# A gated linear attention with a maxout feed-forward on one Trainium2 core: the hand-planned order is planned anew, with the transfers' shared semaphores in the planner and other constants

## The chip, the core and the metric

The kernel runs on one core of one Trainium2 chip. The metric is device time in microseconds (us) of one execution, as the median of the runs shown. Beside it stands the profile of one execution: its span, and what each engine did in it. TensorE is PE (its weight loads are PEld), VectorE is DVE, ScalarE is ACT, GpSimd is POOL, SyncE is SP. SP and ACT are also the two queues that issue transfers.

## The reference

Inputs are `q`, `k`, `v`, `alpha` (batch 4, 8 heads, 768 positions, head dimension 48, float32) and four weight matrices. What is computed:

```python
for t in range(768):                       # per batch and head, state is 48 x 48
    state = alpha[t][:, None] * state + outer(k[t], v[t])
    y[t] = q[t] @ state
x = y as 3072 tokens x 384
h = maximum(maximum(x @ w1, x @ w2), x @ w3)     # 384 -> 768
out = h @ w_out                                  # 768 -> 384
```

## The kernel before, in words

**Units.** The recurrence is done in blocks of 128 positions. A unit u is one block of one batch with all 8 heads; there are 24, block by block, so units 0 to 3 are the first block of the four batches. Inputs are loaded by pairs of units: pair n holds units 2n and 2n+1. For the first four pairs each of a, q, k, v (a is alpha) comes in two half loads of 192 KB, one for each unit of the pair; later pairs come in full loads of 384 KB. In memory the 48 numbers of one position and head are one run of 192 bytes, so these loads consist of small packets.

**A unit's steps.** ACT takes the logarithm of alpha (`la`, L498). PE sums it along the block (L551, one matmul) and ACT makes the two exponentials `ep` and `en` from it (L554, L556). POOL, or DVE where the table `EARLY` says so, forms `qk` = q times ep and k times en (L563); POOL or ACT scales v (L575, L570). PE turns q and k (L533, 8 transposes), DVE copies them out (`qkT`, L537). PE forms the scores (L597, 8 matmuls) and DVE masks them (`LA`, L602). PE forms the outputs from `LA` and v (L643), and, from the second block on, from the carried state `Z` (L640). ACT copies them to `xb` (L651), PE turns them (L665, 3 transposes) and DVE copies them to `xT` (L669). For the last units the two turnings are done by transfers instead: units from `CROSS_IN` on for q and k (L582), from `CROSS_OUT` on for the outputs (L657). The state is carried on by L695 on PE and L701 and L708 on DVE and POOL.

**The feed-forward.** max(x w1, x w2, x w3) is x w1 + max(0, x (w2-w1), x (w3-w1)). So the weights are prepared once: ACT casts w1 and w_out to half precision (L436), POOL or DVE forms the differences `wd` (`subs`, L445; the table `SUBS` says which engine), PE and ACT turn w1 (L463, L469) and PE folds w1 w_out (`folded`, L480, 18 matmuls), which ACT copies (L487). Each matrix comes in two pieces, `WCUTS`: part 0 is 256 columns (384 KB), part 1 is 512 columns (768 KB). For a group of one or two units PE multiplies `xT` by the two differences (L736), ACT takes the positive part (L747), DVE the maximum (L752), and PE multiplies back (L769, 9 matmuls a unit: 3 with the folded matrix, 6 with w_out). ACT copies the result and issues the store (L780, L781). `SINGLE` and `LAST` say how many units at the start and at the end form groups of their own; the others go two by two. One unit alone takes 36 matmuls of 128 columns in L736, two together 36 of 256 columns.

**What sets the order.** Nothing is scheduled by the compiler: every step is entered into `Plan` with an engine, a cost and a rank, and `Plan.order` plays them through (each engine takes the ready step with the earliest start, then the lowest rank), with a small account of transfers (`Transfers`) and of the TensorE clock (`Clock`). The order it finds is emitted as it stands; each engine then runs its own list strictly in order. `FIRST` is the order in which the first loads (`load`, on SP, L406) and the weight pieces (`wload`, on ACT, L427) are asked for. A weight piece is held back in the plan until the load `BACK` + 1 places before it in `FIRST` has landed. `LEAD` holds the ranks of the first feed-forward groups (unit number plus lead).

**The shared semaphores.** The transfers of both queues take eight semaphores in turn, in the order in which they are emitted; call the transfers #0, #1, #2 and so on. Transfer #n waits, on the queue that issues it, until #(n-8) has landed, unless that queue has waited for this already. In the built program before, w3's first piece is #28 on ACT and waits for #20, the k of unit 3. The plan before does not know of this.

Of the kernel before, what the change touches and what calls it, by code (L numbers as in the profile page):

```python
# [25 lines left out]
QUEUES = ("SP", "ACT")  # L26
DMA_IN = {"SP": 0.9, "ACT": 0.9}
DMA_OUT = {"SP": 0.9, "ACT": 0.9}
DMA_BOTH = {"SP": 0.2, "ACT": 0.8}
SPARE = 1.5  # L30
LEAD = (2.5, 8.0, 6.5, 8.0)
EARLY = {0: ("POOL", "POOL", "POOL"), 2: ("POOL", "DVE", "POOL"), 3: ("POOL", "POOL", "POOL"),
         4: ("POOL", "POOL", "POOL"), 5: ("POOL", "POOL", "ACT"), 6: ("POOL", "POOL", "POOL"),
         7: ("POOL", "DVE", "POOL"), 9: ("DVE", "POOL", "POOL"), 10: ("POOL", "POOL", "POOL")}
WCUTS = (0, 256, 768)
SUBS = {(1, 0): "DVE", (1, 1): "POOL", (2, 0): "DVE", (2, 1): "DVE"}
FIRST = (("w", 0, 0), ("a", 0, 1, 2), ("k", 0, 1, 2), ("k", 1, 0, 1), ("q", 0, 0, 1),
         ("q", 0, 1, 2), ("a", 0, 0, 1), ("k", 0, 0, 1), ("a", 1, 0, 1), ("q", 1, 0, 1),
         ("v", 1, 0, 1), ("w", 0, 1), ("w", 1, 1), ("w", 3, 0), ("v", 0, 0, 1), ("w", 1, 0),
         ("w", 3, 1), ("v", 0, 1, 2), ("qav", 1, 1, 2), ("w", 2, 0), ("k", 1, 1, 2),  # L40
         ("w", 2, 1), ("a", 2, 0, 1), ("vk", 2, 0, 1), ("q", 2, 0, 1), ("a", 2, 1, 2),
         ("a", 3, 1, 2), ("vq", 2, 1, 2), ("k", 2, 1, 2), ("a", 3, 0, 1), ("q", 3, 0, 1),
         ("k", 3, 0, 1), ("k", 3, 1, 2), ("q", 3, 1, 2), ("v", 3, 1, 2), ("v", 3, 0, 1))
WARM = (-1, 0, 0)
BACK = 3
SINGLE, LAST = 4, 2
PAIRS, WIDE = 10, 99
CROSS_IN, CROSS_OUT = 22, 18
FETCH, FETCHES, STORE = 1.0, (25.0, 10.2), 0.3
CLOCK_WINDOW, CLOCK_PHASE, CLOCK_WAKE, CLOCK_KEEP = 3.413, 0.0, 0.75, 0.37  # L50

# [70 lines left out]
class Plan:  # L122
# [55 lines left out]
    def order(self):  # L178
# [19 lines left out]
                pending[self.steps[i][0]].add(i)  # L198
        free = dict(dict.fromkeys(HOP, 0.0), SP=SP_FIRST)
        held = {"DVE": 0.0, "POOL": 0.0}  # L200
        bank_free = {b: 0.0 for b in range(NBANKS)}
        place, seq, clock = {}, [], Clock()
        dma, mode, fetch = Transfers(), 0, FETCHES[0]

        def finish(i, done):
            for k in owner.get(i, ()):
                left[k] -= 1
                last[k] = max(last[k], done)
                if not left[k]:
                    for j in range(self.width.get(k, 1)):  # L210
                        bank_free[place[k] + j] = last[k]
            for j in after[i]:
                arrive(j, done)
# [7 lines left out]
        while len(seq) < n:  # L221
            best = None
            for e, cand in pending.items():
                pick = None
                for i in cand:
                    at = self.homes(bank_free, self.steps[i][5])
                    if at is None:
                        continue
                    t = max(ready[i], free[e], at[0])
                    if e == "POOL" or e == "DVE" and self.steps[i][7]:  # L230
                        t = max(t, held["DVE" if e == "POOL" else "POOL"])
                    turn = TURN_RANK if e == "PE" and self.steps[i][7] != mode else 0.0
                    key = (t, self.steps[i][2] + turn, i)
                    if pick is None or key < pick:
                        pick = key
                if pick is not None and (best is None or pick < best[0]):
                    best = (pick, e)
            if best is not None and best[0][0] > fetch:
                dma.store(FETCH)
                fetch += FETCHES[1]  # L240
            landing = dma.next()
            if landing and (best is None or landing[0] <= best[0][0]):
                end, i = dma.next(commit=True)
                self.landed[i] = end
                finish(i, end)
                continue
            (t, _, i), e = best
            _, cost, _, _, _, banks, load, m, late = self.steps[i]
            pending[e].discard(i)
            for k, b in self.homes(bank_free, banks)[1].items():  # L250
                place[k] = b
                for j in range(self.width.get(k, 1)):
                    del bank_free[b + j]
            if e == "PE":
                if m != mode:
                    mode = m
                    cost += TURN_COST
                cost = clock.run(t, cost)
            free[e] = t + cost
            if e == "POOL" or e == "DVE" and m:  # L260
                held[e] = t + cost
            seq.append((t, i))
            if load > 0 and e in QUEUES:
                dma.add(e, t + cost + DMA_IN[e], load, i, late)
            else:
                if load < 0:
                    dma.store(-load)
                finish(i, t + cost + HOP[e])
            if i in follows:
                arrive(follows[i], t)  # L270
# [5 lines left out]
def kernel(  # L276
# [12 lines left out]
    nc = tc.nc  # L289
# [3 lines left out]
    DF = moe_w_out.shape[0]  # L293
# [80 lines left out]
    plan = Plan({x: range(NBANKS) for x in ("Lp", "hp", "tp", "A", "yp", "xp", "pp", "gp", "op", "wt", "wp", "wm")})  # L374
# [23 lines left out]
    asked = []  # L398
# [19 lines left out]
    casting = {g: tuple(x[2] for x in FIRST if x[:2] == ("w", g)) for g in (0, 3)}  # L418
# [3 lines left out]
        return t[:, lo // P:hi // P, :] if g == 3 else t[:, :, lo:hi]  # L422

    def wload(g, part):
        gate = [asked[-1 - BACK]] if len(asked) > BACK else []
        plan.step("ACT", 0.8, -1.0,
                  lambda: nc.scalar.dma_start(  # L427
                      piece(wst[g], g, part),
                      piece(matrices[g].rearrange("(t p) f -> p t f", p=P), g, part)),
                  reads=gate + ([("ws room", p) for p in casting[0]] if g == 3 else []),  # L430
                  writes=[("ws", g, part)], line="weights",
                  load=3.25 * (WCUTS[part + 1] - WCUTS[part]) / DF)
        if g in (0, 3):
            n = NFT * (WCUTS[part + 1] - WCUTS[part])
            plan.step("ACT", 0.2 + 0.00083 * n, -0.5,
                      lambda: nc.scalar.copy(out=piece((w1h, 0, 0, wo16)[g], g, part),  # L436
                                             in_=piece(wst[g], g, part)),
                      reads=[("ws", g, part)],
                      writes=[("w", g, part)] + [("ws room", part)] * (g == 0))
# [277 lines left out]
    def ffn(f, units):  # L717
        k = len(units)
# [6 lines left out]
        for q in range(NJ // span):  # L725
            js = range(q * span, (q + 1) * span)
            parts = sorted({p for j in js for p in parts_of(j // 2)})
            for g in range(2):
                r = rank[2 * q + g]
# [25 lines left out]
        for i in range(k):  # L755
            m = units[i]
# [32 lines left out]
            def leave_left(m=m, ok=ok, rows=rows):  # L789
                nc.scalar.copy(out=obs[m % 4][:, left], in_=live[ok][:, left])  # L790
                nc.scalar.dma_start(rows[:, left], obs[m % 4][:, left])

            plan.step("ACT", 0.7, r, leave_left, reads=[ok], writes=[("ob room", m % 4)])
            plan.step("DVE", 0.3, r,
                      lambda m=m, ok=ok: nc.vector.tensor_copy(out=obs[m % 4][:, right],
                                                               in_=live[ok][:, right]),
# [1 line left out]
            plan.step("SP", 0.4, r,  # L798
                      lambda m=m, rows=rows: nc.sync.dma_start(rows[:, right],
                                                               obs[m % 4][:, right]),  # L800
                      reads=["right"], writes=["done"])


    for what, n, lo, *hi in FIRST:
# [74 lines left out]
```

## Time and profile before

| | |
|---|---|
| time, median of 3 runs | 160.46 us (160.32 to 161.14) |
| time of the profiled execution | 159.96 us |
| its span | 158.2 us |
| busy: PE, DVE, ACT, POOL | 133.3, 94.4, 85.1, 76.4 us |
| loads of q, k, v, alpha | 20.09 MB on SP's queue (with the little that else goes there), 104080 packets |
| weights and stores | 9.44 MB on ACT's queue, 6944 packets |

The span is what the profile shows between the first and the last instruction; 1.8 us of the profiled execution's time lie outside of it. In the rows of the profile, a line such as L736 is a line of the kernel before; "busy, mean ns of one" and the idle time in front of an instruction are given with what ended it. The chain of waits is followed back from the last instruction; its pieces add up to the span.

### The profile page before, as it was taken

The numbers are of one execution on the slowest core, as the hardware profiler recorded it, in microseconds if no ns is written. First come the engines' busy times: TensorE is split into PE (matmuls) and PEld (weight loads), VectorE is DVE, ScalarE is ACT, GpSimd is POOL, SyncE is SP. The second block draws the span as 40 slices with busy tenths as digits, with TensorE's granted clock in tenths as the row PEclk, the third lists the DMA queues.
The fourth block names the chain that finished last, engine by engine and source line by source line (L and its number), as shares of the span: only waits on it lengthen the run. The fifth ranks groups of instructions, "written<-read, shape, count | busy, mean of one in ns | idle before, by whom it ended". The sixth has DMA issues, their size and how long they took to land.

```text
span 158.2 us, 4216 instructions
## 1 busy us (share of the span) xinstructions
PE 133.3 (84%) x1686; PEld 105.8 (67%) x1686; DVE 94.4 (60%) x162; ACT 85.1 (54%) x175; POOL 76.4 (48%) x105
## 2 busy tenths in 40 slices
PE   0217270599999999999999999999999999999991
PEld 0105160596877777869778878869788796979680
DVE  7004640334669898988769957969678750923130
ACT  3355300789378628655865936856748455343330
POOL 0044490100653642969596949699985940000000
PEclk9999999999999999999999999999999999999999
DMA  6999999898999998999989999999521691122121
GB/s 125 255 215 358 227 303 279 205 323 164 199 237 263 205 237 185 234 227 242 230 173 289 181 257 268 176 247 227 110 102 32 59 245 47 57 50 99 54 99 50
DMA packets 111043, 29.80 MB, mean 188 GB/s; under 512 B 104624, under 2 KB 109872, under 8 KB 111024
## 3 DMA queue, kind: packets, MB, share of 16 engines
q1 hardware_dynamic: 104080, 20.09, 66.0%
q10 hardware_dynamic: 6944, 9.44, 18.3%
q8 instruction: 13, 0.21, 0.6%
q14 instruction: 6, 0.05, 0.1%
HBM read 23.69 MB, written 4.72 MB: 180 GB/s over the span
## 4 chain that ended last, share of the span: by engine, by line
PE 71%; SPq 11%; DVE 7%; DMA 6%; issue 2%; ACT 1%; ACTq 0%; DVEq 0%
PE psum L736 29%; PE psum L769 20%; SPq L406 11%; DMA kn<-in_k_dram 6%; PE psum L533 5%; PE psum L597 3%; PE psum L643 3%; DVE LA L602 2%; PE psum L551 2%; PE psum L640 2%; PE psum L480 2%; PE psum L665 2%; PE psum L695 2%; DVE Z L708 2%; DVE qkT L537 1%
## 5 line engine op out<-in xcount | busy, mean ns | idle before, releaser
L736 PE MATMUL psum<-xT,wd 128*128 128x256 f16 (+1 forms) x540 | 55.3, 255 | 0.1
L736 PEld LDWEIGHTS <-wd 128*128 128x128 f16 x540 | 43.9, 100 | 5.1 <-issue 0.5
L563 POOL TENSOR_TENSOR qk<-qn,ep 128x384 f16<-128x384 f32 x23 | 23.0, 1000 | 32.2 <-ACT ep L554 30.3
L602 DVE TENSOR_TENSOR LA<-psum,c 128x1024 f16<-128x1024 f32 x24 | 28.5, 1220 | 12.2 <-PE psum L597 12.2
L752 DVE TENSOR_TENSOR hT<-psum,hT 128x512 f16<-128x512 f32 (+1 forms) x39 | 24.4, 645 | 15.0 <-PE psum L736 9.0
L747 ACT ACTIVATE hT<-psum 128x512 f16<-128x512 f32 (+1 forms) x39 | 21.6, 570 | 18.2 <-PE psum L736 17.7
L769 PE MATMUL psum<-wo,hT 128*128 128x384 f16 x144 | 27.5, 326 | 0.0
L563 POOL TENSOR_TENSOR qk<-kn,en 128x384 f16<-128x384 f32 x22 | 22.4, 1021 | 9.3 <-ACT en L556 9.1
L537 DVE COPY qkT<-psum 128x1024 f16<-128x1024 f16 x22 | 15.1, 688 | 13.4 <-PE psum L533 11.7
L651 ACT ACTIVATE xb<-psum,c 128x384 f16<-128x384 f32 x24 | 13.8, 582 | 16.8 <-DMA kn<-in_k_dram 11.6
L780 ACT COPY ob<-psum 128x384 f32<-128x384 f32 x23 | 11.0, 478 | 20.7 <-PE psum L769 20.7
L769 PEld LDWEIGHTS <-hT 128*128 128x128 f16 x144 | 14.0, 98 | 9.2
L533 PE MATMUL psum<-c,qk 128*128 128x128 f16 x176 | 15.1, 231 | 5.9 <-POOL qk L563 5.9
L708 POOL TENSOR_TENSOR Z<-U,G 48x192 f16<-48x192 f32 x32 | 15.6, 504 | 3.4 <-DVE U L701 2.5
L575 POOL TENSOR_SCALAR v<-vn,c 128x384 f16<-128x384 f32 x23 | 13.8, 603 | 7.0 <-DMA vn<-in_v_dram 6.7
L533 PEld LDWEIGHTS <-qk 128*128 128x128 f16 x176 | 11.5, 103 | 8.3 <-POOL qk L563 7.7
L769 PE MATMUL psum<-w1o,xT 128*128 128x384 f16 x72 | 15.6, 326 | 0.0
L554 ACT ACTIVATE ep<-psum 128x384 f32<-128x384 f32 x24 | 11.9, 494 | 6.2 <-PE psum L551 5.1
L669 DVE COPY xT<-psum 128x384 f16<-128x384 f16 x18 | 6.3, 353 | 10.1 <-PE psum L665 9.9
L556 ACT ACTIVATE en<-psum 128x384 f32<-128x384 f32 x24 | 11.9, 496 | 0.0
L665 PE MATMUL psum<-c,xb 128*128 128x128 f16 x54 | 6.3, 234 | 6.6 <-ACT xb L651 6.6
L643 PE MATMUL psum<-v,LA 128*128 128x48 f16 x192 | 11.6, 188 | 0.1
(41 smaller groups left out, 143.7 us busy)
## 6 DMA issues: line engine op xcount, KB each, us to landing
out_dram<-ob ACTq DMA_DIRECT2D x23, 192.0 KB, 3.1
an<-in_alpha_dram SPq DMA_DIRECT2D x8, 384.0 KB, 5.9
qn<-in_q_dram SPq DMA_DIRECT2D x8, 384.0 KB, 5.7
kn<-in_k_dram SPq DMA_DIRECT2D x8, 384.0 KB, 6.3
vn<-in_v_dram SPq DMA_DIRECT2D x8, 384.0 KB, 6.1
ws<-in_moe_w_dram ACTq DMA_DIRECT2D x3, 768.0 KB, 7.5
an<-in_alpha_dram SPq DMA_DIRECT2D x8, 192.0 KB, 4.9
kn<-in_k_dram SPq DMA_DIRECT2D x8, 192.0 KB, 4.2
```

The costliest lines, as they stand in the source:

```text
L406: nc.sync.dma_start(t[:, lo:hi], views[x][cb * P:(cb + 1) * P, g * HG + lo:g * HG + hi])
L533: nc.tensor.transpose(live[tk][:, w, j, :], qk[:, w, 2 * j:2 * j + 2, :], ident)
L537: plan.step("DVE", 0.69, u, lambda: nc.vector.tensor_copy(out=qkT, in_=live[tk]), reads=[tk], writes=[("qkT", u % 3)])
L563: nc.gpsimd if eng == "POOL" else nc.vector).tensor_mul(
L575: lambda: nc.gpsimd.tensor_scalar(out=v16, in0=ld["v"][n % 5][:, hs], scalar1=vsc, scalar2=1.0, op0=AOP.mult, op1=AOP.mult),
L602: lambda: nc.vector.tensor_mul(LA.rearrange("p a b t -> p (a b) t"), live[Ak].rearrange("p a (b t) -> p (a b) t", t=P), maskA.unsqueeze(1) ...
L643: nc.tensor.matmul(yp[:, 2 * j + p, :], LA[:, p, j, :], v16[:, 2 * j + p, :], start=(cb == 0), stop=True, skip_group_check=True)
L708: eng.tensor_mul(Zn[rows, :, cols], U[rows, :, cols], G[rows, i * NP:(i + 1) * NP].unsqueeze(2).broadcast_to([D, NP, D]))
L736: nc.tensor.matmul(live[gk][:, jj, :], wd[:, kt, g, j * P:(j + 1) * P], xT[:, kt, :], start=(kt == 0), stop=(kt == NFT - 1))
L747: lambda h=h, gk=gk: nc.scalar.activation(out=h, in_=live[gk], func=AFT.Relu),
L752: lambda h=h, gk=gk: nc.vector.tensor_max(h, live[gk], h),
L769: nc.tensor.matmul(live[ok], a[:, i * P:(i + 1) * P], w, start=(kt == 0), stop=(kt == nk - 1))
```

## The change

The planner learns of the eight semaphores: in `Plan.order` a transfer on SP may start only when the sixth transfer before it has landed, one on ACT only when the eighth before it has (`LANES`, `LANDING`); the stores now count as transfers there too. The share of SP's queue beside ACT's is put at 0.17 instead of 0.2. The constants are set anew: other `LEAD`, `EARLY`, `SUBS`, `FIRST`; `SINGLE` 4 to 2 and `LAST` 2 to 4, so that units 0 and 1 and the last four units are groups of their own; `CROSS_OUT` 18 to 21, so that three outputs instead of six are turned by transfers (q and k of two units as before); `WARM` now puts 6 matmuls on zeros onto PE, free to start once the scaled q of unit 2 is there. `WQUEUE` could put the weights on SP's queue, but is "ACT", as before. `BACK` is 2 instead of 3. The steps themselves, their sizes and the buffers stay as they were; the six extra matmuls and nine more transposes are all that PE gets in addition.

```diff
--- before.py
+++ after.py
@@ -26,26 +26,28 @@
 QUEUES = ("SP", "ACT")
 DMA_IN = {"SP": 0.9, "ACT": 0.9}
 DMA_OUT = {"SP": 0.9, "ACT": 0.9}
-DMA_BOTH = {"SP": 0.2, "ACT": 0.8}
+DMA_BOTH = {"SP": 0.17, "ACT": 0.8}
+LANES, LANES_USED, LANDING = {"SP": 6, "ACT": 8}, 2, 2.4
 SPARE = 1.5
-LEAD = (2.5, 8.0, 6.5, 8.0)
-EARLY = {0: ("POOL", "POOL", "POOL"), 2: ("POOL", "DVE", "POOL"), 3: ("POOL", "POOL", "POOL"),
-         4: ("POOL", "POOL", "POOL"), 5: ("POOL", "POOL", "ACT"), 6: ("POOL", "POOL", "POOL"),
-         7: ("POOL", "DVE", "POOL"), 9: ("DVE", "POOL", "POOL"), 10: ("POOL", "POOL", "POOL")}
+LEAD = (6.0, 5.0, 6.0, 8.0)
+EARLY = {2: ("POOL", "POOL", "POOL"), 4: ("POOL", "DVE", "ACT"), 5: ("POOL", "POOL", "POOL"),
+         7: ("DVE", "POOL", "POOL"), 9: ("DVE", "POOL", "POOL"), 10: ("POOL", "DVE", "POOL"),
+         11: ("DVE", "POOL", "ACT")}
 WCUTS = (0, 256, 768)
-SUBS = {(1, 0): "DVE", (1, 1): "POOL", (2, 0): "DVE", (2, 1): "DVE"}
-FIRST = (("w", 0, 0), ("a", 0, 1, 2), ("k", 0, 1, 2), ("k", 1, 0, 1), ("q", 0, 0, 1),
-         ("q", 0, 1, 2), ("a", 0, 0, 1), ("k", 0, 0, 1), ("a", 1, 0, 1), ("q", 1, 0, 1),
-         ("v", 1, 0, 1), ("w", 0, 1), ("w", 1, 1), ("w", 3, 0), ("v", 0, 0, 1), ("w", 1, 0),
-         ("w", 3, 1), ("v", 0, 1, 2), ("qav", 1, 1, 2), ("w", 2, 0), ("k", 1, 1, 2),
-         ("w", 2, 1), ("a", 2, 0, 1), ("vk", 2, 0, 1), ("q", 2, 0, 1), ("a", 2, 1, 2),
-         ("a", 3, 1, 2), ("vq", 2, 1, 2), ("k", 2, 1, 2), ("a", 3, 0, 1), ("q", 3, 0, 1),
-         ("k", 3, 0, 1), ("k", 3, 1, 2), ("q", 3, 1, 2), ("v", 3, 1, 2), ("v", 3, 0, 1))
-WARM = (-1, 0, 0)
-BACK = 3
-SINGLE, LAST = 4, 2
+SUBS = {(1, 0): "POOL", (1, 1): "DVE", (2, 0): "DVE", (2, 1): "POOL"}
+FIRST = (("w", 0, 0), ("k", 0, 1, 2), ("a", 0, 1, 2), ("q", 0, 1, 2), ("vqk", 0, 0, 1),
+         ("a", 0, 0, 1), ("k", 1, 0, 1), ("k", 1, 1, 2), ("a", 1, 0, 1), ("w", 0, 1),
+         ("q", 1, 1, 2), ("w", 3, 0), ("v", 1, 0, 1), ("a", 1, 1, 2), ("w", 1, 1), ("w", 3, 1),
+         ("w", 1, 0), ("v", 1, 1, 2), ("w", 2, 1), ("q", 1, 0, 1), ("w", 2, 0), ("v", 0, 1, 2),
+         ("k", 2, 0, 1), ("a", 2, 0, 1), ("a", 2, 1, 2), ("q", 3, 1, 2), ("a", 3, 1, 2),
+         ("q", 2, 0, 1), ("v", 2, 0, 1), ("k", 2, 1, 2), ("k", 3, 1, 2), ("q", 2, 1, 2),
+         ("v", 3, 1, 2), ("a", 3, 0, 1), ("k", 3, 0, 1), ("v", 2, 1, 2), ("q", 3, 0, 1),
+         ("v", 3, 0, 1))
+WARM = (2, 0, 6)
+BACK, WQUEUE, WTAX = 2, "ACT", 0.3
+SINGLE, LAST = 2, 4
 PAIRS, WIDE = 10, 99
-CROSS_IN, CROSS_OUT = 22, 18
+CROSS_IN, CROSS_OUT = 22, 21
 FETCH, FETCHES, STORE = 1.0, (25.0, 10.2), 0.3
 CLOCK_WINDOW, CLOCK_PHASE, CLOCK_WAKE, CLOCK_KEEP = 3.413, 0.0, 0.75, 0.37
 
@@ -198,6 +200,7 @@
                 pending[self.steps[i][0]].add(i)
         free = dict(dict.fromkeys(HOP, 0.0), SP=SP_FIRST)
         held = {"DVE": 0.0, "POOL": 0.0}
+        lanes, number = [LANDING] * LANES_USED, {}
         bank_free = {b: 0.0 for b in range(NBANKS)}
         place, seq, clock = {}, [], Clock()
         dma, mode, fetch = Transfers(), 0, FETCHES[0]
@@ -229,6 +232,10 @@
                     t = max(ready[i], free[e], at[0])
                     if e == "POOL" or e == "DVE" and self.steps[i][7]:
                         t = max(t, held["DVE" if e == "POOL" else "POOL"])
+                    if self.steps[i][6] and len(lanes) >= LANES[e]:
+                        if lanes[-LANES[e]] is None:
+                            continue
+                        t = max(t, lanes[-LANES[e]])
                     turn = TURN_RANK if e == "PE" and self.steps[i][7] != mode else 0.0
                     key = (t, self.steps[i][2] + turn, i)
                     if pick is None or key < pick:
@@ -241,6 +248,7 @@
             landing = dma.next()
             if landing and (best is None or landing[0] <= best[0][0]):
                 end, i = dma.next(commit=True)
+                lanes[number[i]] = end
                 self.landed[i] = end
                 finish(i, end)
                 continue
@@ -262,9 +270,12 @@
             seq.append((t, i))
             if load > 0 and e in QUEUES:
                 dma.add(e, t + cost + DMA_IN[e], load, i, late)
+                number[i] = len(lanes)
+                lanes.append(None)
             else:
                 if load < 0:
                     dma.store(-load)
+                    lanes.append(t + cost + LANDING)
                 finish(i, t + cost + HOP[e])
             if i in follows:
                 arrive(follows[i], t)
@@ -422,14 +433,16 @@
         return t[:, lo // P:hi // P, :] if g == 3 else t[:, :, lo:hi]
 
     def wload(g, part):
-        gate = [asked[-1 - BACK]] if len(asked) > BACK else []
-        plan.step("ACT", 0.8, -1.0,
-                  lambda: nc.scalar.dma_start(
+        room = [("ws room", p) for p in casting[0]] if g == 3 else []
+        gate = [asked[-1 - BACK]] if len(asked) > BACK and WQUEUE == "ACT" else []
+        plan.step(WQUEUE, 0.5, -1.0,
+                  lambda: (nc.scalar if WQUEUE == "ACT" else nc.sync).dma_start(
                       piece(wst[g], g, part),
                       piece(matrices[g].rearrange("(t p) f -> p t f", p=P), g, part)),
-                  reads=gate + ([("ws room", p) for p in casting[0]] if g == 3 else []),
-                  writes=[("ws", g, part)], line="weights",
-                  load=3.25 * (WCUTS[part + 1] - WCUTS[part]) / DF)
+                  reads=gate + room, writes=[("ws", g, part)],
+                  line="weights" if WQUEUE == "ACT" else "loads",
+                  load=3.25 * (WCUTS[part + 1] - WCUTS[part]) / DF
+                  + (WTAX if WQUEUE == "SP" else 0.0))
         if g in (0, 3):
             n = NFT * (WCUTS[part + 1] - WCUTS[part])
             plan.step("ACT", 0.2 + 0.00083 * n, -0.5,
@@ -790,7 +803,8 @@
                 nc.scalar.copy(out=obs[m % 4][:, left], in_=live[ok][:, left])
                 nc.scalar.dma_start(rows[:, left], obs[m % 4][:, left])
 
-            plan.step("ACT", 0.7, r, leave_left, reads=[ok], writes=[("ob room", m % 4)])
+            plan.step("ACT", 0.7, r, leave_left, reads=[ok], writes=[("ob room", m % 4)],
+                      load=-STORE)
             plan.step("DVE", 0.3, r,
                       lambda m=m, ok=ok: nc.vector.tensor_copy(out=obs[m % 4][:, right],
                                                                in_=live[ok][:, right]),
@@ -798,7 +812,7 @@
             plan.step("SP", 0.4, r,
                       lambda m=m, rows=rows: nc.sync.dma_start(rows[:, right],
                                                                obs[m % 4][:, right]),
-                      reads=["right"], writes=["done"])
+                      reads=["right"], writes=["done"], load=-STORE)
 
 
     for what, n, lo, *hi in FIRST:
```

## The prediction

> **What bounds the kernel now.** I read the page's busy times and slices first, then a table by stage, then the chain of waits and the waits around its first hole.
>
> ```profile
> PE 133.3 (84%) x1686; PEld 105.8 (67%) x1686; DVE 94.4 (60%) x162; ACT 85.1 (54%) x175; POOL 76.4 (48%) x105
> PE   0217270599999999999999999999999999999991
> DMA  6999999898999998999989999999521691122121
> ```
>
> PE is nearly idle for seven slices (28 us) and nearly full from then to the end; the DMA engines are full to 110 us.
>
> ```profile
> 22.80:29.40 6.60, 0.00 (x0) 0.00 (x0) 1.23 (x1) 0.62 (x2) 1.53 (x3) 1.00 1.02 246
> 29.40:38.50 9.10, 8.96 (x101) 7.63 (x102) 4.48 (x6) 8.20 (x15) 0.00 (x0) 1.00 0.99 253
> 51.30:61.50 10.20, 9.81 (x155) 7.48 (x150) 9.37 (x17) 5.56 (x13) 4.42 (x5) 1.00 1.11 224
> 82.00:103.00 21.00, 21.00 (x300) 17.55 (x297) 17.18 (x29) 13.85 (x30) 15.82 (x24) 1.00 1.08 231
> ```
>
> Columns are busy time of PE, PEld, DVE, ACT, POOL, the granted clock, the DMA share and GB/s. From 22.8 to 29.4 no engine works; from 51.3 to 61.5 DVE is full, POOL is not.
>
> ```profile
> 19.31 8.96 DMA kn<-in_k_dram
> 28.29 0.39 ACTq L427
> 28.78 0.59 ACT xb L651
> 38.93 2.01 PE psum L736 x36
> 40.94 1.46 PE psum L769 x9
> ```
>
> The hole is named: k of unit 3 (#20) takes 9 us beside the weights, ACT's issue of w3's first piece (#28) waits for it by the shared semaphore, and xb stands behind that in ACT's list. "ACT xb L651 <- DMA kn" is 11.6 us in the waits.
>
> A busy PE hides waits, so I count its work by the chain's durations at full rate: nine matmuls of L736 for one unit 0.50 us, six for two units 0.66, L769 1.46 a unit, the fold 2.93, turning q and k 0.45, scores 0.275, an xb turned 0.17, L551 0.16, L511 0.18. All of PE's work is 123.8 us. By this count 4.1 us are done before 29.4, 14.2 by 41.9, 34.3 by 64, the rest by 154.8. So PE loses 2.0 us between 41.9 and 64 (22.1 us for 20.1) and 1.3 in the 90.8 us after. What can be won lies before 64 us.
>
> **The change, part by part.** *Where the weights stand.* In the built program ACT issues w_out part 0, w2 part 1, w_out part 1, w2 part 0, w3 part 1, and only then xb of unit 0; w3's last piece is #40, and by the shared semaphore waits for #32, the k of unit 5. Landings I read from the semaphore events of the trace. The first ten transfers are like-sized and land as before (0.88 us apart, to 10.5). ACT issues w1's part 1 at 10.5 instead of 9.69, as the alpha in front of it now comes one place later; it landed 5.48 us after issue, so at 16.0; the cast (1.47) ends at 17.5 and the next weights start. At the intervals of before (4.9 from issue to landing for the first, then 2.0 for 384 KB, 2.4 to 3.6 for 768 KB) they land at 22.4, 25.1, 27.9, 29.9 and 32.9. ACT is free for xb at 25.1 instead of 28.78: 3.6 us earlier. This is what the change gives.
>
> *The new wait.* The DMA engines are full in both kernels, so what has to land before #32 sets its time: 24 half loads and all weights but one 384 KB piece. Before, 24 half loads and all weights had landed at 39.25. Less 1.4 us for that piece (2.0 at a share of some 0.7), #32 lands at 37.9; 36.9 to 38.9, since the share in this stretch is 0.99 to 1.02 and just before 1.11. From issue to landing such a piece took 4.45 us (w1's, 1.67 to 6.12) to 4.84 (w3's, 28.29 to 33.13): 42.6. Its difference on DVE takes 0.95, so PE can start on it at 43.6; ends 42.3 and 44.8.
>
> [...]
>
> Behind #40 in ACT's list wait xb of unit 3, the logarithms of pair 2, and ep and en of units 4 and 5. ACT's steps from 25.1 to there are 9.4 us by their rows (three xb 1.75, one logarithm 0.53, two w1T 1.6, casts 0.84 and 1.47, exponentials 1.26, two positive parts 1.0, two copies of the fold 1.0) with 1.5 of waiting for the fold: it arrives at 36.0 and stands for 1.9 us. What PE has in its list ahead of the first matmul that needs the piece is 14.2 us of work (four units prepared and put out, six groups of nine and two of six, the fold). It gets the xb of units 1 and 2 by 31.2, goes on from 31.4 through 5.9 us to 37.6, stands until 38.5 for the xb of unit 3, and ends its last 3.0 us, with 0.6 of small waits, at 42.1. So the gate costs PE another 1.5 us, and nothing ahead of it matters while it ends by 43.6. PE before had done 14.2 us of work at 41.9. Handicap: +1.75 us (0.3 to 2.9).
>
> *What comes back.* At 43.6 other things are ahead: q and k of unit 5 are scaled at 44.4 (en at 42.2 and two POOL steps of 1.0), against 49.0. Followed on by the rows' durations, every qkT and LA is there 0.1 to 0.7 us before PE comes to it, up to 58 us; but DVE is full from 42.6 to 55, so little slips through. Units 2 and 3 as one group save DVE 0.2 (three maxima of 0.69 for four of 0.56), and it makes one 768-wide difference less (0.95). Of the 2.0 us that PE loses here now, I take 1.2 to come back; ends 0 and 2.0.
>
> *Three more outputs turned on PE.* Nine transposes, three times 0.17: +0.5 us in a stretch where PE is full, so all on the path. The three copies on DVE (0.35 each) are hidden (6.5 of 12 us busy from 125 to 137); uncovered, 1.05. The transfers they replace have no waiter in PE's list of waits: gain 0.
>
> *Moves among engines.* DVE gets two qk (0.55 each) and the three copies, and loses a difference (0.95): +1.2. ACT gets a v (0.63). POOL loses two qk (1.0) and a v (0.6) and gets a difference (half of 3.1): -1.0. From 61.5 to 103 DVE has 8 us of 41 free, ACT and POOL more; cost 0, at the worst 0.6 if PE waits once for the moved v. The large difference of w3 goes from DVE (1.76) to POOL (3.10): landed at 32.9, done at 36.0, wanted by PE at 40.5; hidden, and 3.1 us if that piece were as late as the gate. Six units alone and nine pairs as before: PE's sum is the same (2.01 a unit against 3.94 a pair). The six zero matmuls lie where PE waits for LA of unit 2. The end is built as before: 3.4 us from the last matmul.
>
> **Sum.** 159.96 of the profiled execution + 1.75 - 1.2 + 0.5 = 161.0. That execution is 0.5 under the median of the runs, so 161.5.
>
> **The rivals.** *The preparation pays in full* (faster). Place: 42 to 64 us. If #32 lands by 36.9, the gate opens at 42.3, PE is late by 0.4, all 2.0 come back, and 0.5 goes for the transposes: 160.46 + 0.4 - 2.0 + 0.5 = 159.4. For it: unit 5's lead of 4.6 us, and POOL only 4.4 of 10.2 busy there. Against: DVE is as full as before. It decides at a gate before about 42.7.
>
> *Nothing comes back* (slower). DVE keeps its 2.0 us of holes, as its work up to there is as long: 160.46 + 1.75 + 0.5 = 162.7; with the late end of the gate 163.9.
>
> *PE starts at half rate.* In the chain the first 18 matmuls of L736 take 1.92 us, 107 ns each, and the 36 of 38.93 take 56 ns: PE runs at half rate until about 33.5, 4 us after it starts for good, though the granted clock stands at 1.00 in every row. With a start at 25.8 and the zero matmuls I take full rate from 31. If half rate lasted through those 5.9 us from 31.4, they would end at 43.5, the rest at 47.0 instead of 43.6: up to +3.4, 164.9. It decides only if half rate is still there at 37. [...]
>
> That the order still ignores the semaphores is no rival: the built program names each wait.
>
> **How the numbers follow.** Forecast 161.5 with chance 0.45 (160.6 to 162.4 for itself); paid in full 0.20; nothing back 0.25; half rate 0.05; another course 0.05. A measurement here can tell about 0.5% (0.8 us) from no change: under 159.66 is faster, over 161.26 slower. Of the forecast 0.30 lies above and 0.15 within; of the full payment 0.15 is faster and 0.05 within; the next two are slower; of the last 0.02 is faster and 0.03 within. Faster 0.17, same 0.23, slower 0.60. The range runs from the full payment to nothing back with a gate a little late: 159.3 to 163.3.
>
> **What would show it.** ACT's first xb near 25 and not 28.8; SP's k of unit 5 landing near 38 and ACT standing at its last weight piece until then, after 36; the DVE difference of 128x768 from w3 ending near 43.6, with PE idle for 1 to 2 us in front of it; PE full from there to 59; nine L665 more. Wrong it would be if the last w3 piece came well before 41, if PE lost more than 1 us between 44 and 64, or if a hole opened after 64, where I see none.

## The result and the profile after

The changed kernel takes 161.77 us, median of 20 runs (160.43 to 162.75), against 160.5 for the kernel before on the same chips. The ratio is 1.0095, 95% interval 1.007 to 1.012: slower by about 1.5 us (the two medians alone would give 1.008, or 1.3 us). The ratios here and below leave out the few executions in a slower state of the chip. The prediction was 161.5, its range 159.3 to 163.3. The profiled execution took 162.25 us with a span of 160.3, so it lies 0.5 above its median, as that of before lay 0.5 under its own: between the two traces there are 2.3 us, between the medians 1.3.

Lines of the kernel after L406 stand 11 to 14 further down than before: the weights are issued at L439, the differences are L458, qk is L576, `LA` L615, `xb` L664, its transposes L678, the two large groups of matmuls L749 and L782, the positive part L760, the maximum L765, the zero matmuls L690.

The page first, its busy times and PE's row of slices:

```profile
PE 135.8 (85%) x1701; PEld 106.2 (66%) x1701; DVE 95.8 (60%) x166; ACT 86.1 (54%) x176; POOL 77.8 (49%) x103
PE   0147443997779999999999999999999999999991
```

PE now starts in the seventh slice instead of the eighth, but there is a dent of three slices (36 to 48 us) that the page of before does not have. The table by stage, columns as in the prediction; the last row is the third stage in the kernel before:

```profile
22.80:29.40 6.60, 3.43 (x38) 2.27 (x37) 1.96 (x3) 3.33 (x8) 0.87 (x2) 1.00 1.11 344
29.40:38.50 9.10, 9.07 (x98) 6.41 (x94) 4.87 (x6) 5.06 (x9) 7.89 (x4) 1.00 1.03 235
38.50:51.30 12.80, 9.89 (x113) 7.27 (x113) 8.33 (x16) 8.03 (x19) 4.16 (x4) 1.00 1.05 217
51.30:61.50 10.20, 10.20 (x137) 8.23 (x136) 7.94 (x15) 4.84 (x11) 4.15 (x6) 1.00 1.13 259
38.50:51.30 12.80, 12.68 (x186) 9.93 (x185) 8.81 (x18) 8.40 (x22) 6.45 (x7) 1.00 1.06 226
```

The empty stretch from 22.8 to 29.4 is half filled. From 51.3 to 61.5 PE is full where it had 9.81 of 10.20, and DVE has room (7.94 for 9.37). What was gained at both sides is lost between 38.5 and 51.3: 9.89 of 12.80 us (12.68 before). The waits say for what (time in all, times, longest):

```profile
ACT xb L664 <- DMA ws<-in_moe_w_dram: 7.2, 1, 7.2
ACT xb L664 <- DMA kn<-in_k_dram: 2.2, 1, 2.2
PE psum L749 <- DVE wd L458: 1.3, 1, 1.3
```

The 11.6 us of before ("ACT xb" for "DMA kn") have become 7.2 in front of xb of unit 0 and 2.2 in front of xb of unit 3. The second is the gate of the prediction, and the timeline shows it step by step (start, duration, engine, line; in brackets the idle time in front and what ended it):

```profile
38.69 0.37 ACTq L439 DMA_DIRECT2D ws<-in_moe_w_dram  x1
39.11 0.58 ACT L664 ACTIVATE xb<-psum,c 128x384 f16<-128x384 f32 x1 [2.19 <-DMA kn<-in_k_dram]
39.75 0.34 PE L678 MATMUL psum<-c,xb 128*128 128x128 f16 x3 [1.16 <-ACT xb L664]
42.83 1.00 POOL L576 TENSOR_TENSOR qk<-kn,en 128x384 f16<-128x384 f32 x1 [0.48 <-ACT en L569]
42.93 1.71 DVE L458 TENSOR_TENSOR wd<-ws,w1h 128x768 f16<-128x768 f32 x1 [2.38 <-DMA ws<-in_moe_w_dram]
43.78 1.72 POOL L576 TENSOR_TENSOR qk<-qn,ep 128x384 f16<-128x384 f32 x1
44.57 1.35 DVE L576 TENSOR_TENSOR qk<-kn,en 128x384 f16<-128x384 f32 x1
44.70 0.68 PE L749 MATMUL psum<-xT,wd 128*128 128x128 f16 x9 [1.26 <-DVE wd L458]
46.52 0.81 PE L749 MATMUL psum<-xT,wd 128*128 128x256 f16 x6 [0.30 <-DVE hT L765]
```

k of unit 5 (#32) lands at 38.67; ACT, which stood for it, issues w3's last piece at 38.69 and makes xb of unit 3 behind it. The piece lands at 42.91, DVE starts its difference at 42.93, and PE goes on at 44.70. One thing in these lines was not in the prediction: the difference takes 1.71 us and not 0.95.

Counted as in the prediction (work by the chain's durations at full rate, of 123.82 us before and 124.32 after, or 123.82 where three outputs are turned by transfers), PE had done:

| kernel | by 44 us | by 64 us | span |
|---|---|---|---|
| before | 16.49 | 34.32 | 158.2 |
| changed | 14.18 | 32.38 | 160.3 |
| early | 15.85 | 35.12 | 157.6 |
| hold | 15.24 | 34.58 | 158.1 |
| late | 14.18 | 30.51 | 162.3 |
| before_xb | 18.66 | 35.17 | 157.3 |
| after_xb | 13.53 | 32.47 | 160.2 |
| early_xb | 15.07 | 34.47 | 158.3 |

After 64 us the two go on nearly alike: the changed kernel is 1.94 us of work behind at 64 and has 0.5 more to do, and its span is longer by 2.1. The columns are single profiled executions, which can lie 1 us or more from the median of their kernel (out18's took 161.38, its median is 162.66). The other rows are the experiments.

### The profile page after: what moved, and what is told of

Read it like the earlier page. It is cut to its first block, busy times and chain, and to the rows that moved or that the text cites. A ratio compares the mean times of both kernels' runs of the same rounds, so it can differ in the third digit from the quotient of the medians.

```text
span 160.3 us, 4260 instructions
## 1 busy us (share of the span) xinstructions
PE 135.8 (85%) x1701; PEld 106.2 (66%) x1701; DVE 95.8 (60%) x166; ACT 86.1 (54%) x176; POOL 77.8 (49%) x103
## 4 chain that ended last, share of the span: by engine, by line
PE 69%; SPq 21%; ACT 3%; DMA 2%; DVE 1%; issue 1%; ACTq 0%
PE psum L749 27%; PE psum L782 22%; SPq L417 21%; PE psum L546 5%; PE psum L610 4%; PE psum L656 2%; DMA kn<-in_k_dram 2%; PE psum L653 2%; PE psum L564 2%; PE psum L708 2%; PE psum L678 2%; ACT hT L760 1%; PE psum L524 1%; DVE qk L576 1%; ACT la L511 1%
## 5 line engine op out<-in xcount | busy, mean ns | idle before, releaser
L749 PE MATMUL psum<-xT,wd 128*128 128x256 f16 (+1 forms) x540 | 55.3, 253 | 1.7 <-DVE wd L458 1.3
L749 PEld LDWEIGHTS <-wd 128*128 128x128 f16 x540 | 43.1, 99 | 7.3 <-DVE wd L458 1.5
L615 DVE TENSOR_TENSOR LA<-psum,c 128x1024 f16<-128x1024 f32 x24 | 28.6, 1221 | 11.9 <-PE psum L610 11.1
L765 DVE TENSOR_TENSOR hT<-psum,hT 128x512 f16<-128x512 f32 (+1 forms) x39 | 24.5, 644 | 17.1 <-ACT ob L793 8.8
L576 POOL TENSOR_TENSOR qk<-qn,ep 128x384 f16<-128x384 f32 x21 | 21.7, 1032 | 25.1 <-ACT ep L567 17.0
L760 ACT ACTIVATE hT<-psum 128x512 f16<-128x512 f32 (+1 forms) x39 | 21.8, 572 | 16.8 <-PE psum L749 16.4
L576 POOL TENSOR_TENSOR qk<-kn,en 128x384 f16<-128x384 f32 x22 | 24.1, 1096 | 10.1 <-ACT en L569 9.9
L782 PE MATMUL psum<-wo,hT 128*128 128x384 f16 x144 | 27.5, 326 | 0.0
L664 ACT ACTIVATE xb<-psum,c 128x384 f16<-128x384 f32 x24 | 13.9, 581 | 15.3 <-DMA ws<-in_moe_w_dram 7.2
L782 PEld LDWEIGHTS <-hT 128*128 128x128 f16 x144 | 14.0, 98 | 9.2
L588 POOL TENSOR_SCALAR v<-vn,c 128x384 f16<-128x384 f32 x22 | 12.8, 583 | 12.1 <-DMA vn<-in_v_dram 11.8
L782 PE MATMUL psum<-w1o,xT 128*128 128x384 f16 x72 | 15.6, 326 | 0.0
L682 DVE COPY xT<-psum 128x384 f16<-128x384 f16 x21 | 7.4, 350 | 8.5 <-PE psum L678 5.0
L511 ACT ACTIVATE la<-an 128x384 f16<-128x384 f32 (+1 forms) x16 | 10.9, 680 | 0.9 <-DMA an<-in_alpha_dram 0.9
```

What stands on the lines that cost most here:

```text
L576: nc.gpsimd if eng == "POOL" else nc.vector).tensor_mul(
L615: lambda: nc.vector.tensor_mul(LA.rearrange("p a b t -> p (a b) t"), live[Ak].rearrange("p a (b t) -> p (a b) t", t=P), maskA.unsqueeze(1) ...
L664: lambda: nc.scalar.activation(out=xb, in_=live[yk].rearrange("p a b -> p (a b)"), func=AFT.Copy, scale=ysc),
L749: nc.tensor.matmul(live[gk][:, jj, :], wd[:, kt, g, j * P:(j + 1) * P], xT[:, kt, :], start=(kt == 0), stop=(kt == NFT - 1))
L760: lambda h=h, gk=gk: nc.scalar.activation(out=h, in_=live[gk], func=AFT.Relu),
L765: lambda h=h, gk=gk: nc.vector.tensor_max(h, live[gk], h),
```

## The experiments

Each is compared with the kernel before by the ratio of its runs; the changed kernel is at 1.0095. A ratio less by 0.001 is 0.16 us. Where the intervals of two ratios overlap widely, as with turn18 and after_xb against the changed kernel, the difference between the two is not shown, whatever the medians say. Most edits move steps in the finished order (`seq`), so that the planner's other choices stay as they are.

**early: the gate taken away.** The gate is w3's last piece: its late issue, and what stands behind that issue in ACT's list. The theory: the late gate costs the time. First rival: DVE sets the pace anyway. Step 85 is xb of unit 1.

```diff
     seq, where = plan.order()
+    piece0 = plan.writer[("ws", 2, 0)]
+    seq.remove(piece0)
+    seq.insert(seq.index(85), piece0)
```

> The changed kernel with the issue of w3's 384 KB piece four to eleven places earlier in ACT's list (in front of xb of unit 1 instead of behind the second copy of the fold); all other orders are as they were. It becomes transfer #35 instead of #40 and waits for #27 (landed at 29.7) instead of #32 (38.7). Theory (the late gate sets the time): ACT issues it near 31.4, it lands by 36.5, its difference on DVE is done by 41.5, and PE finds neither the wait of 1.26 us for it at 44.7 nor the 1.16 us for xb of unit 3 at 39.75, which stood behind it, nor the 0.3 at 46.5: 2.7 us, less the 0.9 that the changed kernel already made up by 64 us, so 1.8 under the changed kernel: 160.0 (159.3 to 160.8) where the changed kernel gives 161.8. First rival (DVE, full from 42 to 55, sets the pace in any case): 161.5 to 161.9. Second rival (the loads of SP that now land 1 us later become the next wait): 161.0 to 162.0, with a new wait of PE for qkT of unit 4 or LA before 55 us.

Measured 159.38 us, ratio 0.993 (0.9895 to 0.9965): 2.6 us under the changed kernel, and faster than the kernel before. The timeline:

```profile
30.32 0.38 ACTq L439 DMA_DIRECT2D ws<-in_moe_w_dram  x1
37.63 0.58 ACT L664 ACTIVATE xb<-psum,c 128x384 f16<-128x384 f32 x1 [0.22 <-PE psum L656]
39.62 0.95 DVE L458 TENSOR_TENSOR wd<-ws,w1h 128x768 f16<-128x768 f32 x1
39.76 0.82 PE L749 MATMUL psum<-xT,wd 128*128 128x256 f16 x6 [0.35 <-DVE xT L682]
```

The piece goes out at 30.32, while ACT is still at a copy (L482, 29.84 to 30.66), so that ACT stands for nothing. xb of unit 3 comes 1.5 us earlier, the difference starts without waiting for the transfer and takes 0.95. Between 44 and 64 PE does 19.3 us of work in 20 (before 17.8, changed 18.2). DVE as the pace is out, and no new wait for the later loads of SP came up.

**late: the gate moved the other way.** The same three lines with 131 (the second logarithm of pair 2) for 85, so that xb of unit 3 stands in front of the piece.

> The changed kernel with the same issue three ACT steps later (behind xb of unit 3, a logarithm of pair 2 and one positive part); it becomes #42 and waits for #34 (landed at 40.4) instead of #32 (38.7). Theory (the gate): ACT no longer stands in front of xb of unit 3, but the piece lands near 44.6, the difference is done at 45.6 to 46.3, PE is held there 1.2 to 1.6 us longer than before, and at most half of it comes back: 162.4 to 163.4. First rival (DVE sets the pace): 161.6 to 162.0. Second rival (what costs is ACT standing in front of xb of unit 3, not the piece itself): 1.2 us less, 160.6.

Measured 163.04 us, ratio 1.0185 (1.0135 to 1.0234), 1.4 us more than changed.

```profile
39.93 0.37 ACTq L439 DMA_DIRECT2D ws<-in_moe_w_dram  x1
44.75 0.96 DVE L458 TENSOR_TENSOR wd<-ws,w1h 128x768 f16<-128x768 f32 x1 [6.38 <-DMA ws<-in_moe_w_dram]
45.77 1.14 PE L749 MATMUL psum<-xT,wd 128*128 128x128 f16 x9 [2.74 <-DVE wd L458]
```

xb of unit 3 was made at 36.3, 2.8 us earlier than in the changed kernel, and it did not help; the gate opened 1.07 us later, and that is what counted. So the piece itself costs, and not ACT's standing in front of xb of unit 3. It cost more than the 1.07: behind its stand of 2.74 us PE ran at half rate (the nine matmuls take 1.14 us, 0.68 in the changed kernel; the mean granted clock from 38.5 to 51.3 is 0.87, and 1.00 in the changed kernel), and at 64 this trace is 1.87 us of work behind the changed kernel's.

**hold: POOL kept off the difference.** A copy of one column of `wd` in front of POOL's first qk of unit 4, so that POOL starts its three qk behind the difference.

```diff
+    scrap = sb.tile([P, 1], FP16, name="scrap")
+    (first,) = [i for i in seq if plan.steps[i][:3] == ("POOL", 1.0, 4)]
+    plan.step("POOL", 0.1, 4,
+              lambda: nc.gpsimd.tensor_copy(out=scrap, in_=wd[:, 0, 1, 0:1]))
+    seq.insert(seq.index(first), len(plan.steps) - 1)
```

> The changed kernel with one more POOL step in front of its three qk steps of units 4 and 5: a copy of one column of the wd that DVE's late difference of w3 writes, so that POOL starts them behind the difference instead of beside it. Theory (POOL beside it is what stretches the difference from the 0.95 us of the prediction to 1.71): the difference takes 0.95 to 1.05, the gate opens near 43.9 instead of 44.7, POOL's steps end 1.1 us later, which nobody waits for before 48.6; 0.4 to 0.8 us less than the changed kernel: 161.2. Rival (the difference is slow for another reason, the transfers that land beside it): it stays at 1.5 to 1.75 us, POOL is only later, 161.8 to 162.3.

Measured 160.64 us, ratio 1.0043 (1.0008 to 1.0077): 0.8 us under changed, at the upper end of what was expected; the two intervals just touch.

```profile
41.94 0.96 DVE L458 TENSOR_TENSOR wd<-ws,w1h 128x768 f16<-128x768 f32 x1 [2.34 <-DMA ws<-in_moe_w_dram]
42.82 0.55 DVE L576 TENSOR_TENSOR qk<-kn,en 128x384 f16<-128x384 f32 x1
42.96 0.68 PE L749 MATMUL psum<-xT,wd 128*128 128x128 f16 x9 [0.46 <-DVE wd L458]
43.37 1.00 POOL L576 TENSOR_TENSOR qk<-qn,ep 128x384 f16<-128x384 f32 x1
```

Difference and DVE's qk are back at 0.96 and 0.55, and POOL's qk at 1.00. In this trace #32 landed 0.95 us earlier than in the changed kernel's; from its landing to the gate it is 5.24 us against 6.03, so 0.79 is what POOL had cost up to the gate.

**out18 and turn18: the three outputs.** out18 sets `CROSS_OUT = 18` and lets the planner make the end anew.

> The changed kernel with CROSS_OUT = 18 as before: the outputs of units 18 to 20 are turned by transfers again; nine transposes (0.17 us for three) leave PE, three copies of 0.35 us leave DVE. The order changes from unit 18 on only. Theory of the prediction (PE is full there, nobody waits for those transfers): 0.5 us less, 161.3. Rival (the transfers come late and PE waits for them, or PE had the room): 161.8 or more, up to 162.5.

Measured 162.66 us, ratio 1.0166 (1.0115 to 1.0217): 1.1 us more than changed, so the expectation failed. Its profiled execution took 161.38, the lowest of its six, so the trace can't show the whole loss. The order from unit 18 on was another one, and ended so:

```profile
155.26 0.66 PE L782 MATMUL psum<-wo,hT 128*128 128x384 f16 x3 [0.72 <-DVE hT L765]
```

The last unit's maximum lies open there, a wait that the changed kernel does not have. The clean edit keeps the order:

```diff
         for i in seq:
-            plan.steps[i][3]()
+            eng, cost, u = plan.steps[i][:3]
+            if u in (18, 19, 20) and plan.steps[i][5] == (("xp", u),):
+                cb, b = divmod(u, B)
+                nc.sync.dma_start_transpose(out=xTs[cb % NX][:, :, b * P:(b + 1) * P],
+                                            in_=xbs[u % 5])
+            elif not (u in (18, 19, 20) and (eng, cost) == ("DVE", 0.35)):
+                plan.steps[i][3]()
```

> The changed kernel with its own order kept, in which the outputs of units 18, 19 and 20 are turned by transfers: where the order has the three transposes on PE, SP issues one transposing transfer, and the copy on DVE is left away. (out18 let the planner make a new order from unit 18 on, and ended with a wait of 0.72 us in front of the last three matmuls that the changed kernel does not have.) Theory of the prediction (nine transposes on a full PE cost 0.5 us, nobody waits for the transfers): 0.3 to 0.6 us less than the changed kernel, 161.3. Rival (a transfer needs 2.3 us from issue to landing behind the two long ones of units 22 and 23, and PE comes to a unit before it is there): 0 to 1.0 us more, 161.8 to 162.8.

Measured 160.97 us, ratio 1.0062 (1.0029 to 1.0095): 0.5 us under changed. That agrees with the price that the prediction put on nine transposes, but the two intervals overlap: it is not measured by this. What else out18 lost beside the 0.72 is open.

**early_turn18: both together.**

> early and turn18 together: the w3 piece four to eleven places earlier on ACT, and the outputs of units 18 to 20 turned by transfers. Theory: the two are in different stages and add up: early (0.993 of the kernel before, 159.4) less 0.3 to 0.6 us: 158.9. Rival (the transfers cost PE a wait): 159.4 to 160.4.

Measured 159.12 us, ratio 0.9944 (0.9911 to 0.9977). The expected 0.3 to 0.6 us on top of early can't be seen; with intervals of 0.35% it can't be excluded either.

**before_xb: one issue moved in the kernel before.** w3's first piece (384 KB) behind xb of unit 0 and the copy of w1T; step 39 is the issue of w3's second piece.

```diff
     seq, where = plan.order()
+    piece0 = plan.writer[("ws", 2, 0)]
+    seq.remove(piece0)
+    seq.insert(seq.index(39), piece0)
```

> The kernel before with one edit: ACT issues the first piece of w3 behind xb of unit 0 and the copy of w1T that follows it, instead of in front of them; it becomes transfer #29 instead of #28 and waits for #21 (landed at 22.8) instead of #20 (28.3). Theory (the start and the weights before 64 us are what can be won, and one issue in ACT's list stands for the hole): xb of unit 0 comes near 22 instead of 28.8, the w3 pieces are issued near 23 and 25 instead of 28.3 and 28.8 and land by 33, PE is ahead by 2 to 4 us of work at 40, DVE takes part of it back between 42 and 64: 1.0 to 2.0 us less than before, 159.0. Rival (the DMA engines are full there, what lands earlier pushes something else later): within 0.5 us of before, 160.0 to 160.8.

Measured 160.9 us, ratio 1.0017 (0.9981 to 1.0052): no difference, as the rival had it.

```profile
21.64 0.58 ACT L651 ACTIVATE xb<-psum,c 128x384 f16<-128x384 f32 x1 [3.85 <-PE psum L643]
42.90 0.25 PE L511 MATMUL psum<-c,la 128*128 128x2 f16 x4 [1.14 <-ACT la L498]
45.83 0.33 PE L695 MATMUL psum<-v,qk 128*128 128x96 f16 x4 [0.92 <-ACT e L517]
```

xb of unit 0 came 7.1 us earlier, and by 40 us PE had done 16.81 us of work for 12.54. Then it had nothing to do: it waits for the logarithm, e and qk of the next units, and at 64 it is 0.85 ahead, in a trace that is the fastest of the runs. An earlier start alone was worth nothing.

**nowarm: without the zero matmuls.** The six matmuls of `WARM` are left out of the order; they compute nothing that is used.

> The changed kernel without the six zero matmuls of WARM; nothing else is changed. Theory: they stand where PE has nothing to do, and PE is at full rate by 33 us either way because of its own work from 26 on: 161.5 to 162.1. Rival (PE's half rate lasts longer without them): the first matmuls of L749 stay at 107 ns each until 36 or later, but the gate at 44.7 hides up to 2 us of it: 161.8 to 163.5.

Measured 161.91 us, ratio 1.0105 (1.0071 to 1.0139): the same as changed. The number fits theory and rival; the trace decides for the rival, as the rate in it is another. Six matmuls of 384 columns at the same place of PE's list, first nowarm, then the changed kernel:

```profile
34.75 2.12 PE L493 MATMUL psum<-wo,w1T 128*128 128x384 f16 x6
```

```profile
33.86 1.14 PE L493 MATMUL psum<-wo,w1T 128*128 128x384 f16 x6
```

Without the zero matmuls PE runs at half rate until 36.8, with them until about 33 (eight transposes take 0.61 us at 33.41; in nowarm those at 33.90 take 1.06). The time stays the same because the changed kernel's PE stands later on: in nowarm the piece goes out at 38.36, behind a copy of the fold at 38.35 for which ACT stood 0.96 us on the slow PE, and not on #32; PE then meets neither the 1.16 us in front of xb of unit 3 nor the 1.26 at the difference.

**after_xb, early_xb, early_turn18_xb: an earlier start, with and without the gate.** xb of unit 0 and a logarithm of pair 1 (steps 71, 93) in front of w2's part 0 and w3's part 1.

```diff
+    for i in (71, 93):
+        seq.remove(i)
+        seq.insert(seq.index(34), i)
```

> The changed kernel with xb of unit 0 and one logarithm of pair 1 three weight pieces earlier in ACT's list (behind the second piece of w_out, in front of the first of w2), so that PE can start on unit 0 near 23.6 instead of 26.7. By it w3's last piece becomes #41 instead of #40 and waits for #33 (landed at 39.5) instead of #32 (38.7). Theory (the gate alone decides, what lies ahead of it has room): 0.3 to 0.8 us more than the changed kernel, 162.0 to 162.6, for all that PE starts 3 us earlier. Rival (an earlier start is worth its time): 160.3 to 161.3.

Measured 162.6 us, ratio 1.0122 (1.0077 to 1.0167): not to be told from the changed kernel, and no gain, though PE began to turn the outputs of unit 0 at 22.3 instead of 26.7 and had done 11.17 us of work by 36 for 8.83. All of that was spent in front of the gate:

```profile
38.53 0.37 ACTq L439 DMA_DIRECT2D ws<-in_moe_w_dram  x1
39.59 0.34 PE L678 MATMUL psum<-c,xb 128*128 128x128 f16 x3 [3.30 <-ACT xb L664]
40.45 1.44 PE L749 MATMUL psum<-xT,wd 128*128 128x256 f16 x6
```

The last row shows that the stand cost more than its 3.30 us: behind it PE ran at half rate again (the same six matmuls take 0.81 at 40.61 in the changed kernel; the page's row of the granted clock has 5 in the slice from 40.1 to 44.1 and 9 in all others). So this run does not weigh the gate alone.

> early with the same move of xb of unit 0 and the logarithm; w3's last piece stays #35 and waits for #27. Theory: with the gate gone PE's own pace and the preparation of units 3 to 5 set the time, and ACT's steps behind the weights come 1.1 us earlier: 0.3 to 0.9 us less than early, 158.6 to 159.1. Rival (as in before_xb, the preparation of units 4 and 5 waits for SP's loads, which come no earlier): within 0.3 us of early, 159.2 to 159.7.

Measured 160.51 us, ratio 1.0009 (0.9976 to 1.0043): 1.3 us more than early. That lies outside of both ranges, the theory's and the rival's.

```profile
30.65 1.05 ACT L664 ACTIVATE xb<-psum,c 128x384 f16<-128x384 f32 x2 [2.27 <-DMA ws<-in_moe_w_dram]
31.28 0.81 PE L678 MATMUL psum<-c,xb 128*128 128x128 f16 x6 [2.06 <-ACT xb L664]
34.28 1.89 PE L493 MATMUL psum<-wo,w1T 128*128 128x384 f16 x6
```

ACT reaches the last w3 piece 2 us earlier, and #27, for which it waits, has not landed (30.17): it stands again, now in front of xb of units 1 and 2. PE stands with it for 2.06 us, and its six matmuls of L493 at 34.28 take 1.89 us, at half rate, where early has 1.14. So PE is 0.8 behind early at 44. The 1.3 us are explained by this only as far as 0.65 (the count at 64); the rest is open.

> early, turn18 and the move of xb of unit 0 together. Theory: early_xb less the 0.5 us of nine transposes: 158.2 to 158.7. Rival (neither adds to early): 159.2 to 159.6.

Measured 160.35 us, ratio 0.9967 (0.9925 to 1.0009), between early_turn18 and early_xb and above both ranges; ACT stands there, too (2.07 us in front of xb of unit 1).

The best version is early, 0.7% under the kernel before.

## Why the prediction was right, by its own steps

*What bounds the kernel.* "No engine works" between 22.8 and 29.4 holds for PE alone: the row beside it has 1.23 us of DVE, 0.62 of ACT and 1.53 of POOL. Nothing in the sum rests on it.

*Where the weights stand.* Right in order, most of them 0.3 to 1.4 us later than predicted: w1's part 1 landed at 17.4 (16.0), w_out part 0 at 23.2 (22.4), w2 part 1 at 25.6 (25.1), w_out part 1 at 28.2 (27.9), w2 part 0 at 29.7 (29.9), w3 part 1 at 34.2 (32.9). xb of unit 0 came at 26.07 (25.1). What the sentence "this is what the change gives" claims for the early start is too much: in before_xb and after_xb a start 4 to 7 us earlier alone gave nothing. What the change gives shows up in early, with its start at 26.6, between 44 and 64 us; that it is the preparation of units 3 to 5 is argued from the order of the steps and was not tested by itself.

*The new wait.* #32 landed at 38.67 (37.9, range 36.9 to 38.9), the piece 4.2 us after its issue, at 42.91 (42.6).

*The term that was mis-sized* is "its difference on DVE takes 0.95, so PE can start on it at 43.6". It took 1.71, and the gate opened at 44.70. The handicap was 2.84 us instead of 1.75, 0.3 of the excess from the landing and 0.8 from the difference. The prediction looked at what waits for the piece, and not at what runs beside its difference: two qk on POOL, whose ep and en ACT makes behind the same issue, so that the gate makes them late together with it. The rows show what happens then. POOL's qk ends at 43.83, and 0.95 more is 44.78; DVE ended at 44.64. POOL's next qk, listed from 43.78, ends at 45.50, 1.0 after 44.5. So by these rows the difference on DVE and the qk on POOL did not run side by side at reduced speed (POOL's first qk kept its 1.00): the second stood until the first was done, to within 0.14 us, and its listed duration includes the standing. hold, which keeps POOL away, brings the difference back to 0.96.

Which instruction stands depends on where the landing falls. In turn18 the difference took 1.39. In out18 and nowarm, with the same late gate, it took 0.96, but there the DVE steps behind it met POOL: its qk took 1.36 and 1.35 and a step of 0.15 took 0.96 in both, and PE stood for the maximum behind them (0.92 and 0.89). So it is in nowarm:

```profile
43.50 1.35 DVE L576 TENSOR_TENSOR qk<-kn,en 128x384 f16<-128x384 f32 x1
46.25 0.81 PE L749 MATMUL psum<-xT,wd 128*128 128x256 f16 x6 [0.89 <-DVE hT L765]
```

From the piece's issue to this group of PE, the first for two units behind the gate, there are 7.83 us in the changed kernel, 7.88 in turn18, 7.91 in out18 and 7.89 in nowarm, but 6.57 in hold. The collision costs these traces 1.3 us, wherever it falls; the 0.8 of the difference is a part of it. By its runs hold is 0.8 us faster than the changed kernel.

*What comes back.* 1.2 us were forecast. At 64 the changed kernel is 1.94 behind, so 0.9 of the 2.84 came back. "PE full from there to 59" did not hold, and one of the signs of being wrong that the prediction named was there: PE lost 1.8 us between 44 and 64 (18.2 of work in 20), 0.7 of it before the gate at 44.70 and 1.1 behind it. The other signs held: no hole came after 64, the piece did not come before 41, and PE stood 1.26 us in front of the difference.

*Three outputs.* +0.5, and turn18 gives 0.5, within the noise.

*The sum* with the measured terms is 159.96 + 2.84 - 0.9 + 0.5 = 162.4, and the profiled execution took 162.25. But the number came out in part by luck. The prediction added 0.5 to get from the profiled execution to the median; the changed kernel's profiled execution lies 0.5 above its median instead. So the traces lose 2.3 us where the sum had 1.05, and the medians only 1.3. Why the medians lose less is open: the runs without a profile don't show it.

*The rivals.* "The preparation pays in full" was put at 159.4, with the point of decision at a gate before 42.7. early has the difference done at 40.6 and takes 159.38, but that the two numbers are alike is partly chance: of the 2.2 us that PE loses between 44 and 64 in the kernel before, 1.4 come back in early, not all. The point of decision does not hold up either: in out18's trace the gate opened at 42.4, and PE stood 0.92 us for the next maximum all the same. "Nothing comes back" (162.7) is out by the 0.9 us. "PE starts at half rate" did not decide, but nowarm, early_xb and after_xb show that it is real, and in late and after_xb it came back behind a stand of PE (2.74 and 3.30 us), which the prediction did not consider. In nowarm PE works without a break from 32.0 and is at full rate from 36.8, 4.8 us later.

One thing in the document's first part has to be put more exactly. The shared semaphores are taken in the order of the built program, and that is not the planner's order of the two queues. In the planner's own list for the changed kernel w3's last piece is #32, issued at 30.95, and by its account the piece waits for #24; in the built program it is #40 and waits for #32 (landed at 38.67, the piece issued at 38.69). So the planner knew of the semaphores, but counted eight transfers too few in front of this piece.

## What to carry to other kernels

Where two queues share a ring of semaphores, as here, the place of a transfer in the built program decides what it waits for (w3's last piece went out at 38.69 us as #40, behind #32, and at 30.32 as #35, behind #27): list it, and look for a transfer with work behind it that waits for one just issued. Moving one issue by a few places was worth 2.6 us here, and moving an early start by 4 to 7 us was worth nothing, because PE stood for the next thing instead. When a step is made late, look at what becomes late together with it, and whether the two can run side by side (the difference took 1.71 us beside POOL's qk and 0.96 without it).

## What was not expected of the hardware

- DVE and POOL steps on two operands took turns in the changed kernel's trace: DVE's 128x768 difference 0.96 alone and 1.71 beside POOL, its qk 0.55 and 1.35, POOL's qk 1.00 and 1.72 (alone: hold). By the ends of these rows the duration in the profile includes the standing.
- The granted clock can stand at 1.00 in the rows of the table while PE runs at half rate: six matmuls of 384 columns took 2.12 us in nowarm, whose page has 9 in every slice of that clock, and 1.14 in the changed kernel. In the changed kernel the trace's records of the clock begin at 33.1 and in the kernel before at 33.75; the row from 22.8 to 29.4, which lies ahead of both, shows 1.00 (eight transposes at 22.50 in the changed kernel took 1.03 us). Eight transposes took 0.61 us at 31.81 in hold, 32.04 in turn18, 32.57 in late, 33.41 in the changed kernel and 34.06 in out18, and 1.06 at 33.90 in nowarm.
- Later a fall back to half rate does show in the granted clock, in late (mean 0.87 from 38.5 to 51.3) and in after_xb (5 in the slice from 40.1 to 44.1), behind stands of PE of 2.74 and 3.30 us. Behind one of 1.81 us in hold there was none (1.00 from 38.5 to 51.3); in before_xb the mean was 0.74 from 22.8 to 29.4, where PE stood 1.05 and 0.87 us.
- Between the profiled executions of kernels with the same front the issue that waits for #32 moved from 37.11 (out18) to 38.69 us (the changed kernel), and the end of the difference with it, from 42.35 to 44.64.
